# Two more row fetches at the end of an expert loop: rows of the conditional tiles fetched by the last two tiles that always run

## The chip, the cores and the metric

The kernel runs on one core of one Trainium2 chip. The metric is the time of one launch on the device in microseconds (us), as the median over runs. The kernel before takes 700.07 us (three runs, 700.06 to 700.40). One execution of it was recorded by the hardware profiler; its span, from the first to the last instruction, is 698.1 us.

The engines are named as in the profile: PE is the matrix engine, PEld its loads of stationary operands, DVE the vector engine, ACT the scalar engine, POOL the GpSimd engine, SP the engine that issues most transfers. A name with q at its end (POOLq) is that engine's instruction sequencer, which deals with branches, semaphores and the issuing of transfers.

## What is computed

A block-sparse attention is followed by a mixture of experts. Each of the 3072 tokens goes to one of 8 experts, which multiplies it by two weight matrices.

```python
# attention: out = softmax(scale * q k^T, masked by blocks) v   (B=4, H=8, S=768, D=64)
x = attn_out.transpose(0, 2, 1, 3).reshape(3072, 512)

xn = x / (norm(x) + 1e-6);  en = expert_emb / (norm(expert_emb) + 1e-6)
logits = xn @ en.T / tau
expert_idx = argmax(logits, axis=1)
gate_w = softmax(logits)[arange(N), expert_idx]
for e in range(8):
    mask = expert_idx == e
    h = maximum(x[mask] @ w1[e], 0.0)               # w1[e]: 512 x 1024
    out[mask] = gate_w[mask, None] * (h @ w2[e])    # w2[e]: 1024 x 512
```

How many tokens an expert gets is known only on the chip, once the attention has been computed.

## The kernel before

The attention writes each token's row, with its gate, into a table `x_dram` in the chip's main memory. The table has N+1 rows of 4 x 129 float32 values; row N is zero. The tokens are then sorted into tiles of 128 rows that all belong to one expert. There are three kinds of tiles, numbered in the order in which they run:

- tiles 0 to 4 (NE = 5) are early: they use tokens of the first two sequences;
- tiles 5 to 24 (FULL = 20) always run. Two of them are mixed: their halves belong to two experts;
- tiles 25 to 28 (up to NL = 24 late tiles in all) run only if the routing needs them. They stand in a block that the program enters by a test on the chip.

So 25 tiles always run. In the recorded execution 25 tiles ran and no more (23 whole and 2 mixed).

`fetch_rows` gathers the rows of one tile. For a late tile it is four indirect transfers, issued by POOL, each of which brings one quarter row (129 values, 516 bytes) to each of the 128 partitions. Four buffers `xg` are used in turn. The transfers are placed behind the latest output transfer (`k.scattered`) on POOL. A lane of a tile that has no token has the index of row N.

```python
def fetch_rows(k, i):
    late = int(i >= NE)
    x = ring(k, "xg", i, 4, k.wp, [P, ND, XE])              # 4 buffers in turn
    t = ORDER[i - NE] if late else i
    ...
        behind = k.scattered if late else k.squared
        if behind is not None:
            order.enter_context(k.tc.issue_after(behind))
        if late:
            quarters = k.x_dram.rearrange("n (e w) -> (n e) w", e=ND)
            for g in range(NG):                              # NG = 4
                k.nc.gpsimd.indirect_dma_start(              # L828
                    out=x[:, g], out_offset=None, in_=quarters,
                    in_offset=bass.IndirectOffsetOnAxis(ap=k.quarter[:, g, t:t + 1], axis=0), ...)
    ...

def fetch(k, i):
    if i + 2 < k.stop and i + 2 != NE:                       # k.stop is NE + FULL = 25
        fetch_rows(k, i + 2)
    need = [(t, at) for t in range(k.stop) for at in parts(t)]
    ...                                                      # then the weights of coming tiles, on SP
```

A tile's computation is two chains of matmuls with a clamp at zero between them. The first half of `h` is clamped by ACT, the second by DVE. Then the rows of the next tile are turned by DVE, and the result goes out by an indirect transfer on POOL.

```python
def expert_tile(k, i, meanwhile=None, then=None):
    ...
    for f0 in (0, half):
        for f in range(half):
            for d in range(ND):
                nc.tensor.matmul(hp[:, f, :], ...)                      # L907
        if f0 == 0:
            nc.scalar.activation(h[:, 0:half], hp, ACT.Relu)            # L910
        else:
            k.relu = nc.vector.tensor_scalar(out=h[:, half:NF], in0=hp, ..., op0=ALU.max).ins   # L914
    if i + 1 < k.stop:
        prepare(k, i + 1)                                               # L888 to L893, DVE
    for f in range(NF):
        nc.tensor.matmul(yp, lhsT=h[:, f, :], rhs=w2[:, f, :], ...)     # L922
    finish(k, i, yp, gate, slot)

def finish(k, i, yp, gate, slot):
    nc.vector.tensor_scalar(out=y, in0=yp, scalar1=gate, ..., op0=ALU.mult)         # L930
    k.scattered = nc.gpsimd.indirect_dma_start(out=k.out[:, :], ..., in_=y[:, :])   # L931
```

Around them stand the loop, the conditional tiles and the end of the program:

```python
def expert_tiles(n, ...):
    n.stop = NE + FULL
    for i in range(NE + FULL):
        ...
        fetch(n, i)
        ...                                  # mixed_tile(n, i) or expert_tile(n, i)

def last_tiles(n):                           # stands inside more(n)
    used = n.nc.values_load(n.used[0:1, 0:1], min_val=0, max_val=NL)
    for i in range(FULL, NL):
        more.enter_context(n.tc.If(used > i))
        n.stop = NE + i + 1
        fetch_rows(n, NE + i)
        ...                                  # weights, prepare, expert_tile

    # the end of the program
    fast(n)                                  # attention and expert_tiles
    todo = n.nc.values_load(n.todo[0:1, 0:1], min_val=0, max_val=2)     # L1240
    with tc.If(todo > 0):                                               # L1241
        more(n)        # last_tiles, and an exact version of everything (it has expert_tiles too)
    # L1270: the end of the program's context, where all engines meet
```

## Time and profile before

| | before |
|---|---|
| time, median of three runs | 700.07 us |
| span of the recorded execution | 698.1 us |
| PE busy | 679.2 us, 97% of the span |
| POOL busy | 289.7 us, 42% |
| DVE busy | 343.4 us, 49% |
| gathers of late rows (L828) | 80, 1006 ns each on POOL |
| output transfers (L931) | 25, about 1.01 us each on POOL |
| late whole tile | 14.0 us, from the start of one to the next |
| last matmul ends | 681.2 us after the start |

The span is read in three pieces. Up to about 320 us the attention runs. Then 25 tiles follow, one after the other; the last two that always run begin at 653.15 us and 667.17 us. From 681.2 us on no matmul runs: the last result is scaled and sent out, the block of the conditional tiles is jumped over, and the engines meet. A late whole tile is 7.14 us of L907 and 6.87 us of L922 on PE, back to back.

An indirect transfer has two times in the trace. One is the busy time on POOL[...]. The other ends later, when the data has landed and a semaphore is raised.

### The profile page before, as it was taken

How to read it: one execution, taken by the hardware profiler on the slowest of the kernel's cores; microseconds unless marked ns; L12 is line 12 of the kernel's file. 1: busy time of each engine (PE TensorE's matmuls, PEld its weight loads, DVE VectorE, ACT ScalarE, POOL GpSimd, SP SyncE). 2: the span in 40 equal slices, each digit the busy share in tenths (PEclk: the TensorE clock that was granted, in tenths of full speed). 3: DMA queues.
4: the chain of work that ended last, by engine and by line, in shares of the span. 5: the costliest groups of instructions: out<-in, count | busy, mean ns of one | idle time of the engine just before them, and what ended most of it. 6: DMA issues, size and time to landing. Idle time of an engine off the chain costs nothing.

```text
span 698.1 us, 19311 instructions
## 1 busy us (share of the span) xinstructions
PE 679.2 (97%) x8221; PEld 427.0 (61%) x8221; DVE 343.4 (49%) x734; ACT 188.5 (27%) x266; POOL 289.7 (42%) x442
## 2 busy tenths in 40 slices
PE   9999999999999999999999999999999999999990
PEld 4555555555555555557667776674667746677660
DVE  7887778787888888865752112111221122111200
ACT  5455545554555545552000000000000000000000
POOL 1255466544774468626302442244323432234000
PEclk9999999999999999999999999999999999999995
DMA  7833345674426569644999899999899998999300
GB/s 119 138 66 53 49 65 70 131 179 83 69 50 160 119 158 201 234 152 154 350 402 378 306 335 344 349 320 337 317 399 402 401 376 322 399 407 397 110 18 14
DMA packets 170023, 155.91 MB, mean 223 GB/s; under 512 B 129148, under 2 KB 129148, under 8 KB 167110
## 3 DMA queue, kind: packets, MB, share of 16 engines
q1 hardware_dynamic: 163366, 141.47, 65.4%
q0 software_dynamic: 4960, 12.90, 5.0%
q8 instruction: 66, 1.08, 0.7%
q10 hardware_dynamic: 1600, 0.20, 0.2%
q14 instruction: 31, 0.25, 0.1%
HBM read 138.74 MB, written 16.07 MB: 222 GB/s over the span
## 4 chain that ended last, share of the span: by engine, by line
PE 96%; DMA 1%; DVE 0%; issue 0%; ACT 0%; POOL 0%; POOLq 0%
PE hp L907 24%; PE yp L922 23%; PE sc L371 22%; PE av L393 18%; PE back L428 3%; PE hp L950 2%; PE yp L970 2%; PE back L421 2%; DMA kld<-in_k_dram 0%; PE hp L962 0%; DMA qld<-in_q_dram 0%; PE xg_ps L883 0%; PE slot_ps L669 0%; ACT e L374 0%; PE quarter_ps L686 0%
## 5 line engine op out<-in xcount | busy, mean ns | idle before, releaser
L374 ACT ACTIVATE e<-sc 128x768 f32<-128x768 f32 x192 | 155.7, 811 | 147.0 <-PE sc L371 143.3
L907 PEld LDWEIGHTS hp<-xgt,w 128*128 128x128 f32 x1472 | 167.8, 192 | 10.8 <-issue 10.2
L907 PE MATMUL hp<-xgt,w 128*128 128x128 f32 x1472 | 169.3, 275 | 0.0
L922 PE MATMUL yp<-w,h 128*128 128x512 f32 x368 | 161.7, 592 | 0.0
L371 PE MATMUL sc<-qt,kt 64*64 64x384 f32 x1536 | 158.0, 482 | 0.1
L393 PE MATMUL av<-e,vld 64*64 64x384 f32 x1536 | 154.1, 486 | 0.0
L390 DVE TENSOR_TENSOR esum<-esum,e 128x768 f32<-128x768 f32 x128 | 128.2, 1002 | 32.3 <-ACT e L374 29.1
L922 PEld LDWEIGHTS yp<-w,h 128*128 128x128 f32 x368 | 68.2, 190 | 77.0 <-issue 75.8
L456 POOL TENSOR_TENSOR sq<-sq 128x192 f32<-128x192 f32 (+1 forms) x186 | 103.5, 557 | 13.9
L910 ACT ACTIVATE h<-hp 128x512 f32<-128x512 f32 x23 | 13.7, 597 | 290.8 <-PE hp L907 264.0
L828 POOL DMA_INDIRECT xg<-x_dram,quarter x80 | 80.5, 1006 | 28.1 <-issue 23.2
L931 POOL DMA_INDIRECT out_dram<-y,slot_l x20 | 20.1, 1007 | 169.1 <-DVE y L930 169.1
L914 DVE TENSOR_SCALAR h<-hp 128x512 f32<-128x512 f32 x23 | 15.9, 692 | 147.8 <-PE hp L907 147.8
L393 PEld LDWEIGHTS av<-e,vld 64*64 64x64 f32 x1536 | 55.1, 133 | 53.6 <-issue 26.5
L371 PEld LDWEIGHTS sc<-qt,kt 64*64 64x64 f32 x1536 | 58.8, 133 | 38.9 <-issue 36.0
L452 POOL TENSOR_TENSOR sq<-x 128x384 f32<-128x384 f32 x31 | 30.8, 993 | 112.4 <-DVE part L441 96.5
L371 PE MATMUL sc<-qmask,kmask 64*64 64x384 bf16 x768 | 65.9, 323 | 0.1
L930 DVE TENSOR_SCALAR y<-yp,gate 128x512 f32<-128x512 f32 x20 | 15.0, 751 | 83.5 <-PE yp L922 71.4
L371 PEld LDWEIGHTS <-kmask 64*64 64x64 bf16 x768 | 24.7, 107 | 33.0 <-issue 33.0
L388 DVE TENSOR_TENSOR esum<-e 128x768 f32<-128x768 f32 x32 | 31.4, 981 | 7.1 <-ACT e L374 7.1
L428 PE MATMUL back<-ones,esum 64*64 64x1 f32 x1536 | 26.4, 190 | 0.0
L428 PEld LDWEIGHTS back<-ones,esum 64*64 64x64 f32 x1536 | 25.6, 135 | 0.0
(206 smaller groups left out, 354.8 us busy)
## 6 DMA issues: line engine op xcount, KB each, us to landing
w<-in_moe_w_dram SPq DMA_DIRECT2D x50, 2048.0 KB
w<-in_moe_w_dram SPq DMA_DIRECT2D x16, 512.0 KB
x_dram<-x SPq DMA_DIRECT2D x24, 258.0 KB
vld<-in_v_dram SPq DMA_DIRECT2D x32, 192.0 KB
kld<-in_k_dram SPq DMA_DIRECT2D x60, 96.0 KB
qld<-in_q_dram SPq DMA_DIRECT2D x60, 96.0 KB
x_early<-x SPq DMA_DIRECT2D x12, 258.0 KB
xg<-x_dram,quarter POOLq DMA_INDIRECT x80
```

The costliest lines, as they stand in the source:

```text
L371: nc.tensor.matmul(ps[D * r:D * (r + 1), h, 0:HALF], lhsT=rows[D * h:D * (h + 1), keys], rhs=cols[D * h:D * (h + 1), queries], start=first ...
L374: k.exps = nc.scalar.activation(e, ps[:, :, 0:HALF], ACT.Exp, scale=SCALE)
L388: k.summed = nc.vector.tensor_tensor(out=k.esum, in0=k.first, in1=e, op=ALU.add)
L390: k.summed = nc.vector.tensor_tensor(out=k.esum, in0=k.esum, in1=e, op=ALU.add)
L393: nc.tensor.matmul(k.av[D * h:D * (h + 1), r, 0:HALF], lhsT=v[D * r:D * (r + 1), h, kc, :], rhs=e[D * r:D * (r + 1), h, :], start=(kc == 0 ...
L428: nc.tensor.matmul(sums[D * s:D * (s + 1), t, h, r:r + 1], lhsT=esum[D * r:D * (r + 1), h, cols], rhs=k.ones[D * r:D * (r + 1), 0:1], star ...
L452: nc.gpsimd.tensor_tensor(out=sq, in0=x, in1=x, op=ALU.mult)
L456: k.squared = nc.gpsimd.tensor_tensor(out=out, in0=sq[:, :, 0:width], in1=sq[:, :, width:2 * width], op=ALU.add).ins
L828: k.nc.gpsimd.indirect_dma_start(out=x[:, g], out_offset=None, in_=quarters, in_offset=bass.IndirectOffsetOnAxis(ap=k.quarter[:, g, t:t + ...
L907: nc.tensor.matmul(hp[:, f, :], lhsT=w1[:, d, (f0 + f) * P:(f0 + f + 1) * P], rhs=xt[:, d, :], start=(d == 0), stop=(d == ND - 1))
L922: nc.tensor.matmul(yp, lhsT=h[:, f, :], rhs=w2[:, f, :], start=(f == 0), stop=(f == NF - 1))
L931: k.scattered = nc.gpsimd.indirect_dma_start(out=k.out[:, :], out_offset=bass.IndirectOffsetOnAxis(ap=slot, axis=0), in_=y[:, :], in_offse ...
```

## The change

Tile i fetches the rows of tile i+2. Before, the test `i + 2 < k.stop` left this out for the last two tiles that always run (23 and 24), for tiles 25 and 26 do not always run. The change takes this test away, so that tiles 23 and 24 fetch the rows of the conditional tiles 25 and 26. It is for the case that these tiles run: their rows would then be on the way already. `last_tiles`, which the diff leaves as it is, still fetches the rows of each conditional tile when that tile runs.

```diff
 def fetch(k, i):
 
-    if i + 2 < k.stop and i + 2 != NE:
+    if i + 2 != NE:
         fetch_rows(k, i + 2)
     need = [(t, at) for t in range(k.stop) for at in parts(t)]
     begin = [t for t, _ in need].index(i)
```

The same function is used in the exact version inside the block that is jumped over, so eight gathers are added there as well.

## The prediction

> **What bounds the kernel now.** I read the chain that ended last first, restricted to the stretch from 600 us to the end. Columns: start in us, length in us, engine, what it wrote, line, count.

> ```profile
> 639.14 7.14 PE hp L907 x64
> 646.29 6.87 PE yp L922 x16
> 653.15 7.14 PE hp L907 x64
> 660.30 6.87 PE yp L922 x16
> 667.17 7.14 PE hp L907 x64
> 674.31 6.88 PE yp L922 x16
> 681.20 0.03 issue
> 681.22 0.76 DVE y L930
> 681.98 0.03 issue
> 682.01 0.50 POOLq L1240
> 682.52 0.70 POOL out_dram L931
> ```

> Each piece begins where the one before ends: through tiles 22, 23 and 24 the end is set by matmuls alone, 14.01 us per tile, with no gap. The change touches tiles 23 (from 653.15) and 24 (from 667.17). After 681.2 us the chain leaves PE.

> Next I read POOL in order of time, for that is the engine that gets work. In brackets stands its idle time before the instruction.

> ```profile
> 640.21 1.01 POOL L931 DMA_INDIRECT out_dram<-y,slot_l  x1 [7.76 <-DVE y L930]
> 641.52 1.03 POOL L828 DMA_INDIRECT xg<-x_dram,quarter  x1 [0.30 <-issue]
> 642.85 1.00 POOL L828 DMA_INDIRECT xg<-x_dram,quarter  x1 [0.30 <-issue]
> 644.16 1.00 POOL L828 DMA_INDIRECT xg<-x_dram,quarter  x1 [0.30 <-issue]
> 645.46 1.00 POOL L828 DMA_INDIRECT xg<-x_dram,quarter  x1 [0.30 <-issue]
> 654.23 1.01 POOL L931 DMA_INDIRECT out_dram<-y,slot_l  x1 [7.77 <-DVE y L930]
> 668.24 0.99 POOL L931 DMA_INDIRECT out_dram<-y,slot_l  x1 [13.01 <-DVE y L930]
> 682.25 0.97 POOL L931 DMA_INDIRECT out_dram<-y,slot_l  x1 [13.02 <-DVE y L930]
> ```

> Tile 22 shows the pattern that tiles 23 and 24 will get: an output transfer, then four gathers in 6.25 us (from 640.21 to 646.46), then idle time. In tiles 23 and 24 POOL now sits idle for 13 us.

> Last I read the end of the program, by the instructions of its lines L1241 and L1270. Columns after the name: count, shortest, median and longest duration in ns, first and last start in us.

> ```profile
> L1241 POOLq COMPARE_BRANCH  x1: 53/53/53, 682.6 to 682.6; - x1
> L1241 POOLq INC_SWDGE_SEM  x1: 2388/2388/2388, 685.8 to 685.8; - x1
> ...
> L1270 POOLq DRAIN  x3: 40/107/9061, 688.2 to 697.8; - x3
> ```

> The last 15 us are POOL's: the branch over the conditional block at 682.6, nothing until about 685.2, 2.4 us in an instruction that adjusts the semaphores of POOL's transfers, then a drain of 9.06 us, from 688.2 to 697.3. All other engines wait for it; 0.8 us later the span ends.

> [...] output transfers stand at 0.97 to 1.01 us on POOL, and by the landing records the one that starts at 654.23 lands at 656.98 and the one at 682.25 at 685.15. [...]

> **The change, part by part.** It removes nothing that runs. It adds eight gathers, four in tile 23 and four in tile 24; those in the block that is jumped over never run.

> *POOL.* Eight gathers of 1.006 us (mean of L828) with 0.30 us between: 8 x 1.31 = 10.5 us, in two stretches of 5.2 us. The first runs from 654.23 + 1.31 = 655.5 to 660.5, the second from 669.5 to 674.5. The output transfer of tile 24 comes at 682.25, so 7.7 us of idle time remain. On the path: 0.

> *Buffers.* Tiles 25 and 26 take the buffers of tiles 21 and 22, whose rows DVE turned one tile ahead (that of tile 22 at 634.1 us). No wait.

> *Landing.* Tile 22's gathers take 5.2 to 5.9 us from their start to their landing, while weights are streaming too (DMA share 0.73 between 640 and 654 us). In tiles 23 and 24 the share is 0.05 and 0.06. Even at 5.9 us the last one, starting at 673.5, lands at 679.4, before the last output transfer is issued at 682.25. On the path: 0.

> *DVE.* Here something does move.

> ```profile
> 647.52 0.69 DVE L914 TENSOR_SCALAR h<-hp 128x512 f32<-128x512 f32 x1 [7.59 <-PE hp L907]
> 660.34 0.69 DVE L914 TENSOR_SCALAR h<-hp 128x512 f32<-128x512 f32 x1 [6.39 <-PE hp L907]
> 674.35 0.69 DVE L914 TENSOR_SCALAR h<-hp 128x512 f32<-128x512 f32 x1 [6.39 <-PE hp L907]
> ```

> In tile 22 the clamp starts 1.23 us after its matmuls end (646.29), in tiles 23 and 24, which have no gathers, 0.04 us after. The earlier late tiles with gathers are like tile 22: the clamp starts 0.99 to 1.10 us after the last gather's end on POOL. So DVE seems to be held by the gathers, and with them the clamps of tiles 23 and 24 should start at about 661.5 and 675.5. Does PE notice? It needs the second half of h from the ninth of the sixteen matmul records of L922: in tile 24 at 674.31 + 8 x 0.43 = 677.7. The clamp would end at 675.5 + 0.69 = 676.2. 1.5 us of slack remain, and tile 22, with its late clamp, shows L922 at the same 6.87 us. On the path: 0. The rows of tile 24, turned behind that clamp, are ready at about 663.4 instead of 662.3, and are needed at 667.17.

> *The end of the program.* Here alone I can't work out a zero. If the 2.39 us and the 9.06 us are a fixed price, nothing is added. If they grow with the number of indirect transfers (110 have run by then: 5 + 80 gathers and 25 outputs), each has a share of 11.45/110 = 0.104 us, and eight more cost 0.83 us. The profile speaks for neither, as there is one such drain in it. I give proportional growth one chance in four: 0.2 us. Sum: 700.07 + 0.2 = 700.3 us.

> **The rivals.** (1) *The end grows with the transfers*: 700.9 us. For it: that an idle engine drains for 9 us needs a cause, and POOL alone has one. Against it: the last transfer has landed at 685.15, three microseconds before the drain starts. (2) *The late clamp stalls PE* for what exceeds its slack: tile 22 speaks against it. If the gathers were 2 us longer, PE would lose 0.5 us in each of two tiles: 701.1 us. (3) *The gathers land late and hold up the last output transfer.* Tiles 25 and 26 are empty, so all 128 lanes read the same row N, at four addresses. If that made a gather several times slower, the last output would land later; up to 685.5 us, where POOL looks at the semaphores, it costs nothing, beyond that one for one: 702 us would need a landing 2 us late. Against it: an otherwise idle DMA. (4) *A gain.* The rows are wanted only by a block that is jumped over, and even there they are fetched again. Nothing becomes shorter[...].

> **Range and chances.** The nearest alternatives lie between 700.07 and 701.1, and the three runs lie within 0.34 us. Range: 699.7 to 701.3 us. A change of 2% is 14 us, as much as a whole tile; no rival comes near. Faster by over 2%: 0.01; within 2%: 0.97; slower by over 2%: 0.02.

> **What would show it.** Right: 88 gathers at L828, the new ones near 655.5 to 660.5 and 669.5 to 674.5; clamps at about 661.5 and 675.5; PE's pieces in the chain unchanged and the last L922 ending at 681.2. The end then decides: a drain of 9.06 us says fixed price, one of 9.7 with a semaphore step of 2.55 says proportional. Wrong: a gap in the chain before L922 or L907 in tile 24 (rival 2), POOL's semaphore step well after 685.8 (rival 3), or an output transfer of tile 24 that starts later than 682.3, which I hold to be impossible by the idle time that remains on POOL.

## The result, and the profile after

The changed kernel takes 690.39 us (690.3 to 690.79, four runs) against 700.1 us before: a ratio of 0.9861, with a 95% interval of 0.9846 to 0.9875. The recorded span falls from 698.1 to 688.5 us. The time falls by 9.7 us, for a change that only adds work. The prediction was 700.3 us, with a range from 699.7 to 701.3.

First the chain that ended last, from 639 us on, in the changed kernel (start in us, length in us, engine, what it wrote, line, count):

```profile
639.37 7.14 PE hp L907 x64
646.51 6.87 PE yp L922 x16
653.38 7.14 PE hp L907 x64
660.53 6.87 PE yp L922 x16
667.40 7.14 PE hp L907 x64
674.54 6.88 PE yp L922 x16
681.42 0.03 issue
681.45 0.76 DVE y L930
```

Every piece has the length it had before. All of them stand 0.22 to 0.23 us later, and that shift is there already at 604 us, fifty microseconds ahead of the first added gather. So the tiles brought neither gain nor loss.

Now POOL in order of time (idle time before each instruction in brackets), in the changed kernel:

```profile
654.45 1.01 POOL L931 DMA_INDIRECT out_dram<-y,slot_l  x1 [7.77 <-DVE y L930]
655.76 1.02 POOL L828 DMA_INDIRECT xg<-x_dram,quarter  x1 [0.31 <-issue]
...
659.70 1.00 POOL L828 DMA_INDIRECT xg<-x_dram,quarter  x1 [0.31 <-issue]
668.47 1.01 POOL L931 DMA_INDIRECT out_dram<-y,slot_l  x1 [7.77 <-DVE y L930]
671.55 1.02 POOL L828 DMA_INDIRECT xg<-x_dram,quarter  x1 [2.08 <-issue]
672.88 1.00 POOL L828 DMA_INDIRECT xg<-x_dram,quarter  x1 [0.31 <-issue]
...
682.48 1.01 POOL L931 DMA_INDIRECT out_dram<-y,slot_l  x1 [6.00 <-DVE y L930]
```

The added gathers stand where they were expected, with one exception that is easily passed over: the first gather of tile 24 starts at 671.55, after 2.08 us of idle time where the other added gathers have 0.30 or 0.31. Counted from the start of the program it is POOL's 114th indirect transfer.

Last the end of the program in the changed kernel (count, then shortest, median and longest duration in ns, first and last start in us):

```profile
L1241 POOLq COMPARE_BRANCH  x1: 53/53/53, 682.8 to 682.8; - x1
L1241 POOLq INC_SWDGE_SEM  x1: 428/428/428, 686.2 to 686.2; - x1
...
L1270 POOLq DRAIN  x3: 40/107/1057, 686.7 to 688.3; - x3
```

Here is the whole gain. The semaphore step falls from 2.388 to 0.428 us (-1.96) and the drain (the longest of the three) from 9.061 to 1.057 us (-8.00); the prediction shows both lines of before. Against that the step begins 0.41 us later (0.23 us of it the early shift). Together -9.55 us, of the 9.6 us by which the span fell.

### The profile page after: what moved, and what is told of

Read it like the earlier page. It is cut to its first block, busy times and chain, and to the rows that moved or that the text cites. A ratio compares the mean times of both kernels' runs of the same rounds, so it can differ in the third digit from the quotient of the medians.

```text
span 688.5 us, 19327 instructions
## 1 busy us (share of the span) xinstructions
PE 679.6 (99%) x8221; PEld 427.1 (62%) x8221; DVE 343.0 (50%) x734; ACT 188.5 (27%) x266; POOL 297.6 (43%) x450
## 4 chain that ended last, share of the span: by engine, by line
PE 99%; DVE 0%; ACT 0%; issue 0%; POOL 0%; POOLq 0%
PE hp L907 24%; PE yp L922 23%; PE sc L371 22%; PE av L393 18%; PE back L428 3%; PE yp L970 2%; PE hp L950 2%; PE back L421 2%; PE warm L82 1%; PE hp L962 0%; PE xg_ps L883 0%; PE slot_ps L669 0%; ACT e L374 0%; PE quarter_ps L686 0%; DVE y L930 0%
## 5 line engine op out<-in xcount | busy, mean ns | idle before, releaser
L907 PEld LDWEIGHTS hp<-xgt,w 128*128 128x128 f32 x1472 | 167.8, 192 | 10.8 <-issue 10.2
L907 PE MATMUL hp<-xgt,w 128*128 128x128 f32 x1472 | 169.3, 275 | 0.0
L922 PE MATMUL yp<-w,h 128*128 128x512 f32 x368 | 161.7, 592 | 0.0
L922 PEld LDWEIGHTS yp<-w,h 128*128 128x128 f32 x368 | 68.2, 190 | 77.0 <-issue 76.0
L828 POOL DMA_INDIRECT xg<-x_dram,quarter x88 | 88.3, 1004 | 32.3 <-issue 27.4
L914 DVE TENSOR_SCALAR h<-hp 128x512 f32<-128x512 f32 x23 | 15.9, 691 | 149.3 <-PE hp L907 149.3
L931 POOL DMA_INDIRECT out_dram<-y,slot_l x20 | 20.1, 1007 | 157.0 <-DVE y L930 157.0
L930 DVE TENSOR_SCALAR y<-yp,gate 128x512 f32<-128x512 f32 x20 | 15.0, 751 | 82.3 <-PE yp L922 70.2
```

What stands on the lines that cost most here:

```text
L828: k.nc.gpsimd.indirect_dma_start(out=x[:, g], out_offset=None, in_=quarters, in_offset=bass.IndirectOffsetOnAxis(ap=k.quarter[:, g, t:t + ...
L907: nc.tensor.matmul(hp[:, f, :], lhsT=w1[:, d, (f0 + f) * P:(f0 + f + 1) * P], rhs=xt[:, d, :], start=(d == 0), stop=(d == ND - 1))
L922: nc.tensor.matmul(yp, lhsT=h[:, f, :], rhs=w2[:, f, :], start=(f == 0), stop=(f == NF - 1))
```

## The experiments

**The theories.** *Theory 1, a list that fills.* A transfer of POOL stays on a list even after it has landed. 113 transfers of 128 lanes fit; the one that does not fit clears the list. The semaphore step and the drain at the end walk what is still on it. The kernel before ends with 110 on it, three short of a clearing; the changed one clears it with its 114th transfer and ends with five. *Theory 2, recent work.* POOL's end is short if it has had gathers shortly before. *Theory 3, moved code.* The added instructions move the place to which POOL branches.

**Three gathers more, and four.** The two kernels differ in a single gather, one that nobody reads.

```diff
-    if i + 2 < k.stop and i + 2 != NE:
-        fetch_rows(k, i + 2)
+    some = range({23: 3, 24: 0}.get(i, NG))          # three more; the other kernel has 23: 4
+    if i + 2 != NE and len(some):
+        fetch_rows(k, i + 2, some)                   # only the quarters in some
```

> The kernel before with three more gathers, all in tile 23 (three of the four quarters of tile 25): 113 indirect transfers in all. In the changed kernel the first gather of tile 24, the 114th transfer, starts 1.8 us later than the pattern of the other tiles says. Theory 1, a list that fills: each transfer stays on a list after it has landed; 113 fit, the 114th clears it, and the last semaphore step and the drain walk what is on it. From the two kernels (110 on the list: 2.39 and 9.06 us; 5 on it: 0.43 and 1.06 us) a transfer costs 0.0187 us in the step and 0.0762 us in the drain, beside 0.335 and 0.676 us fixed. Here nothing is cleared: step 2.45 us, drain 9.3 us, time about 700.4 us. Theory 2, recent work: gathers shortly before the end make POOL's end short. The gathers lie 22 us before the end: a drain clearly under 9 us if 22 us is still recent, 9.06 us if not. Theory 3, moved code: the added instructions move the place to which POOL branches: a short drain, about 691 us.

> One gather more than the kernel with three: 114 transfers, the last of them the output of tile 24. Theory 1: this output clears the list, and is itself the only entry: the output is held up by some 1.8 us, the semaphore step takes 0.35 us, the drain 0.75 us; time 691.1 to 691.5 us. Theories 2 and 3: as with three more gathers, within 0.3 us, whichever value that has.

With three the time is 700.87 us (ratio 1.0007, 0.9998 to 1.0016), with four 691.71 us (0.988, 0.9864 to 0.9897). The end of the program with three more gathers:

```profile
L1242 POOLq INC_SWDGE_SEM  x1: 2448/2448/2448, 686.4 to 686.4; - x1
...
L1271 POOLq DRAIN  x3: 40/107/9306, 688.9 to 698.7; - x3
```

And with four:

```profile
L1242 POOLq INC_SWDGE_SEM  x1: 348/348/348, 687.3 to 687.3; - x1
...
L1271 POOLq DRAIN  x3: 40/107/731, 687.7 to 689.0; - x3
```

One more gather shortens the end by 2.1 + 8.6 us, and the durations are within 0.02 us of those that theory 1 gave. Recent work would have treated the two alike, for their gathers lie in the same tile, and so would moved code, short of a single instruction deciding. The price of clearing is seen on POOL in the kernel with four, where the 114th transfer is the last output:

```profile
668.14 1.01 POOL L932 DMA_INDIRECT out_dram<-y,slot_l  x1 [7.76 <-DVE y L931]
683.63 1.00 POOL L932 DMA_INDIRECT out_dram<-y,slot_l  x1 [14.47 <-issue]
```

It starts 2.51 us after its result's scaling on DVE begins (681.12), where the changed kernel needs 1.03 us (681.45 to 682.48). So the clearing costs 1.48 us here (1.8 were expected), on the path. In the changed kernel it cost 1.77 us (2.08 less 0.31), but off the path: the gather that paid it had idle time around it.

**The same eight, early.** The eight added gathers go to tiles 7 and 8 and to a buffer of their own.

```diff
+def extra(k, i, lanes=P):
+    spare = ring(k, "spare", 0, 1, k.wp2, [P, ND, XE])
+    ...                                   # behind k.scattered, like fetch_rows
+        for g in range(NG):
+            k.nc.gpsimd.indirect_dma_start(out=spare[0:lanes, g], ...)   # rows of tile i, a second time
 def fetch(k, i):
     if i + 2 < k.stop and i + 2 != NE:
         fetch_rows(k, i + 2)
+    if i in (7, 8) and not k.exact:
+        extra(k, i, P)
```

> The eight added gathers lie in tiles 7 and 8, some 260 us before the end, and go to a buffer of their own that nobody reads: 118 transfers, tiles 23 and 24 have no gathers. Theory 1: the 114th is the third gather of the rows of tile 24, in tile 22; it starts 1.8 us late with no effect on PE; five on the list at the end: step 0.43 us, drain 1.06 us, time 690.4 us. Theory 2: nothing recent, drain 9.06 us, time 700.1 us. Theory 3: open, 690 to 700 us.

It takes 690.37 us (0.9861, 0.9845 to 0.9878), as the changed kernel does. The end of it:

```profile
L1257 POOLq INC_SWDGE_SEM  x1: 428/428/428, 685.9 to 685.9; - x1
...
L1286 POOLq DRAIN  x3: 40/107/1057, 686.4 to 688.0; - x3
```

To the nanosecond the durations of the changed kernel, with nothing recent in tiles 23 and 24. Theory 2 is out. Its 114th transfer, the third gather in tile 22, starts only 0.19 us late (0.49 us of idle time where its neighbours have 0.30), not the expected 1.8: POOL was in the middle of a run of gathers there, and most of the clearing seems to pass beside them.

**Forty fewer.** To see whether the list has a price below 113, the gathers of ten tiles are left out. These tiles compute with the rows that are still in their buffers.

```diff
-        if late:
+        if late and not 15 <= i < 25:
...
-        else:
+        elif not late:
```

> The gathers of tiles 15 to 24 are left out (these tiles compute with the rows that are still in their buffers, so their results are left out): 40 fewer, 70 transfers, nothing cleared. Theory 1: step 0.335 + 70 x 0.0187 = 1.64 us, drain 0.676 + 70 x 0.0762 = 6.01 us, time about 700.1 - 3.8 = 696.3 us. Theory 2: less recent work than before, so no shorter: 9.06 us, 700.1 us. A clearing that is all or nothing, without a price per transfer: 9.06 us as well.

Measured: 696.41 us (0.9946, 0.993 to 0.9963). Both durations are 3 to 4% below the expected ones:

```profile
L1241 POOLq INC_SWDGE_SEM  x1: 1588/1588/1588, 686.0 to 686.0; - x1
...
L1270 POOLq DRAIN  x3: 40/107/5794, 687.7 to 694.0; - x3
```

The price per transfer is real, and a little higher than expected. Against the kernel before, 40 gathers fewer take 800 ns off the step and 3267 ns off the drain: 20.0 and 81.7 ns each, where theory 1 had 18.7 and 76.2. Three gathers more gave the same prices (60 and 245 ns), and so do two and five entries after a clearing (0.368 and 0.812 us in a kernel shown below, 0.428 and 1.057 us in the changed one). The line of theory 1 was too flat because it joined a kernel that had cleared its list to one that had not, and the two kinds are set apart. At 20.0 and 81.7 ns the kernels that never clear end as if seven of their transfers were not on the list (103 for 110 before, 63 for 70 here), in the step and in the drain alike. Whether seven have left it earlier, or the fixed part is smaller as long as nothing has been cleared, no run tells.

**Eight of 16 lanes, and twenty.** What fills the list, the number of transfers or their pieces?

```diff
+    if i in (23, 24) and not k.exact:
+        extra(k, i, 16)                  # the second kernel: ten of them in each of the two tiles
```

> As the changed kernel, but the eight added gathers in tiles 23 and 24 fetch only 16 lanes each instead of 128 and go to a buffer of their own: 118 transfers, eight of them of an eighth of the size. Theory 1a, the list holds so many transfers, whatever their size: the 114th clears it, step 0.43 us, drain 1.06 us, 690.4 us. Theory 1b, the list is filled by the pieces of the transfers: 110 full ones and eight small ones stay below what 113 full ones take, so nothing is cleared: step 2.39 to 2.54 us, drain 9.06 to 9.7 us, 700.1 to 700.8 us. Theory 2, recent work: eight recent gathers, drain near 1.06 us.

> Ten gathers of 16 lanes in each of tiles 23 and 24, to a buffer of their own: 130 transfers. Eight such gathers did not clear the list, where eight full ones do. If a narrow one takes an eighth of the room of a full one, 110 + 20/8 = 112.5 stays below the 113 that fit, nothing is cleared, and 130 entries are walked: step 2.77 us, drain 10.6 us. If a narrow one takes a fifth or more (a share for each transfer beside the share for its lanes), 110 + 4 = 114 or more do not fit, and the last transfers clear the list: step under 0.45 us, drain under 1.1 us. The time itself is not asked for: the gathers may hold DVE up.

With eight the time is 701.3 us (1.0014, 1.0007 to 1.002). Its end has 118 transfers, as many as the changed kernel, and no clearing:

```profile
L1257 POOLq INC_SWDGE_SEM  x1: 2548/2548/2548, 686.5 to 686.5; - x1
...
L1286 POOLq DRAIN  x3: 46/107/9709, 689.0 to 699.3; - x3
```

So the pieces fill the list, while the walk is charged by the transfer, small ones included: against the kernel before, eight narrow ones add 160 and 648 ns, 20 and 81 ns each. With twenty narrow ones the list is cleared:

```profile
L1257 POOLq INC_SWDGE_SEM  x1: 381/381/381, 706.0 to 706.0; - x1
...
L1286 POOLq DRAIN  x3: 46/107/807, 706.4 to 708.2; - x3
```

That is about two entries, so the last narrow gather cleared it (0.38 us of idle time before it, 0.30 or 0.31 before the others), and a narrow transfer takes more than an eighth of the room of a full one. It is not the bytes that fill the list: the twenty bring 165 KB and clear it, the three full gathers more bring 198 KB and do not. The kernel with twenty took 710.26 us in one run: the clamps of tiles 23 and 24 start 9.7 us late, after ten gathers in a row, and PE waits for them; its time says nothing about the end.

**Seventy-two more.** Does the list fill again?

```diff
+    if i in range(5, 23) and not k.exact:
+        extra(k, i, P)
```

> In each of tiles 5 to 22 four more gathers go to a buffer of their own that nobody reads: 182 transfers. Theory 1: the 114th clears the list, and it fills again: 182 - 113 = 69 on it at the end: step 0.335 + 69 x 0.0187 = 1.63 us, drain 0.676 + 69 x 0.0762 = 5.93 us; with POOL hiding the added 5.2 us per tile, time about 690.4 + 6.1 = 696.5 us. A list that is cleared one by one once it has been full would stay at 113: drain 9.3 us, 700.4 us. More work on POOL by itself, without a list: 690.4 us or whatever the added data cost.

The end behaves as a list that has filled again:

```profile
L1257 POOLq INC_SWDGE_SEM  x1: 1715/1715/1715, 725.8 to 725.8; - x1
...
L1286 POOLq DRAIN  x3: 40/107/6284, 727.6 to 734.4; - x3
```

At 20.0 and 81.7 ns, counted from the changed kernel with its five entries, that is 5 + 1287/20.0 = 69.4 and 5 + 5227/81.7 = 69.0 entries: the 69 that were expected. The durations themselves were expected at 1.63 and 5.93 us, by the flatter line. The 114th transfer, a gather in a run of gathers, has no more idle time before it (0.30 us) than its neighbours. The time missed by far: 735.84 us (1.0499, 1.0466 to 1.0532). The chain of that kernel, in one tile, shows where it went:

```profile
608.99 7.34 PE hp L923 x64
616.34 3.44 PE yp L938 x8
619.77 2.72 issue
622.49 3.70 PE yp L938 x8
```

PE stops after the eighth record of the second matmul chain: it waits for the second half of h. DVE in that stretch ("remote" stands where the profile found no releaser on this core):

```profile
609.07 0.75 DVE L946 TENSOR_SCALAR y<-yp,gate 128x512 f32<-128x512 f32 x1 [6.07 <-PE yp L986]
621.75 0.69 DVE L930 TENSOR_SCALAR h<-hp 128x512 f32<-128x512 f32 x1 [11.93 <-remote]
```

The clamp could have started when its matmuls ended, at 616.34, and started at 621.75, after the last of eight gathers in a row had ended on POOL (at 621.55):

```profile
620.55 1.00 POOL L868 DMA_INDIRECT spare<-x_dram,quarter  x1 [0.30 <-issue]
```

This is rival 2 of the prediction, at 4.0 to 5.5 us of delay per tile in place of 1.2. PE stops in 16 tiles, for 1.3 to 2.8 us each, about 29 of the 40 us by which its last matmul ends later than before; the rest is in longer pieces (3.70 for 3.44 us behind the stop above, and 6.72 us in one tile, where the granted clock was 0.79).

Eight gathers in a row do not always hold the clamp. The kernel with eight early gathers has them in tiles 7 and 8; in tile 8 (POOL, DVE, and PE's piece of the chain):

```profile
445.98 1.00 POOL L828 DMA_INDIRECT xg<-x_dram,quarter  x1 [0.30 <-issue]
447.28 1.00 POOL L868 DMA_INDIRECT spare<-x_dram,quarter  x1 [0.30 <-issue]
446.85 0.69 DVE L930 TENSOR_SCALAR h<-hp 128x512 f32<-128x512 f32 x1 [6.39 <-PE hp L923]
446.81 6.87 PE yp L938 x16
```

The clamp starts 0.04 us after its matmuls, in the middle of gathers that last from 442.05 to 452.19, and PE does not stop. In this trace, and in those of the kernels with three and four more and with forty fewer, no clamp of a whole late tile is late. These four were taken on one chip, and the traces with late clamps whose chip is on record on two others. Whether the chip decides or something else was not tried, so the cause of the late clamps stays open, and the 735.84 us may belong to the chip as much as to the kernel.

**Five more, beside the changed kernel.** A kernel in which the clearing falls on the last gather ahead of the last output, so that only two transfers are left.

```diff
+    some = range({23: 4, 24: 1}.get(i, NG))
```

> Five of the eight added gathers: four in tile 23, one in tile 24. 115 transfers; the 114th is the gather in tile 24, so the list is cleared where POOL is idle, and only that gather and the last output are on it at the end. Theory 1: step 0.335 + 2 x 0.0187 = 0.37 us, drain 0.676 + 2 x 0.0762 = 0.83 us, 0.3 us less than the changed kernel with its five on the list; time 690.1 us. If the shortening needs all eight gathers, or the four in the last tile: between 690.4 and 700.1 us.

> The changed kernel once more, on the chip that runs the kernel with five gathers, so that a few tenths can be told: 690.4 us; step 0.43 us and drain 1.06 us, if these depend on the count alone.

They take 690.69 us (0.9864, 0.9847 to 0.988) and 690.61 us (0.9864, 0.9848 to 0.9881): no difference. The step and the drain are as short as expected, 0.368 and 0.812 us, but something else ends last now. In the kernel with five:

```profile
L1242 DVEq EVENT_SEMAPHORE  x2: 21/21/21, 685.5 to 688.0; - x2
...
L1271 POOLq EVENT_SEMAPHORE  x4: 17/17/17, 688.5 to 689.2; - x4
```

POOL's drain is over at 687.81, and the engines meet only at 688.5, as DVE, between its two semaphore instructions behind the branch, pauses from 685.5 to 688.0. In the changed kernel run again the two stand at 685.1 and 685.2. With the drain gone, the end is short enough for such a pause on another engine to show. The kernels with three, four and five gathers more, whose code differs in those counts alone, all have it (2.3 to 2.6 us), and no other kernel has. What sets it was not tried.

## Why the prediction was wrong

## What to carry to other kernels

Where a program ends in a long drain on POOL (9.06 us here), count its indirect transfers: in these runs the end was paid by the transfers left on the list since it was last cleared, 0.102 us each, and a few idle transfers that move the clearing close to the end, where POOL is idle, were worth 9.7 us here. The price was a sawtooth: one transfer more, the 114th, took 9.2 us off the time, and with 72 more transfers, 69 of them on the list at the end, a step of 1.715 us and a drain of 6.284 us were back, so look at the count after each change. And look at DVE beside a run of gathers: in the run with 72 more, where the clamp started only after the last of eight gathers, 4.0 to 5.5 us late with a slack of 1.5 us by the estimate in the prediction, PE stopped for 1.3 to 2.8 us in each of 16 tiles.

## What the runs showed that was not expected

- Landed transfers still cost: 20.0 ns each in the semaphore step and about 81.7 ns each in the drain. The step alone would not have drawn attention; the drain is four times as dear.
- The clearing costs 1.48 us on the path, 1.77 us where POOL is otherwise idle, and 0 to 0.19 us in the middle of a run of gathers.
- DVE's clamp starts 4.0 to 5.5 us late beside eight gathers in a row on POOL in one kernel and 0.04 us late in another, 9.7 us late beside ten narrow ones, and in tiles with four gathers either 0.04 or about 1.2 us late. That the gathers can hold it is the reading; what passes between the two engines, and when, stays open.
